# Sums of squares of expert weights moved from ScalarE to GpSimd, and a row of schedule edits, in a one-core attention and PEER kernel

## The chip, the core and the metric

The kernel runs on one core of a Trainium2 chip. TensorE (PE) multiplies matrices into PSUM and takes its stationary operand by a separate weight load (PEld); VectorE (DVE), ScalarE (ACT) and GpSimd (POOL) work element by element on 128 partitions; SyncE (SP) issues most DMAs, and GpSimd issues the indirect ones (gathers). Each engine runs its own instructions in the order in which the program lists them, and semaphores hold an instruction until what it needs is there. The metric is the device time of one execution in microseconds.

## What is computed

```python
def reference(A_x, A_wq, A_wk, A_wv, A_wo, B_x, B_w_q, B_k1, B_k2, B_u, B_v):
    ...                                   # x: 1 x 2048 x 512, 32 heads
    x = A_x
    xn = _layernorm(x, axis=-1)
    return x + _A_ref(xn, A_wq, A_wk, A_wv, A_wo) + _B_ref(xn, B_w_q, B_k1, B_k2, B_u, B_v)

def _A_ref(...):                          # attention, 32 query heads of 16, one key and value head
    scores = jnp.einsum("bhqd,bkd->bhqk", q, k) * (Dh ** -0.5)
    p = _softmax(scores, axis=-1)
    o = jnp.einsum("bhqk,bkd->bhqd", p, v)
    return o ... @ wo

def _B_ref(...):                          # product-key experts, N = 64 * 64 = 4096, D = 512
    q = jnp.einsum("nd,dhc->nhc", xf, w_q)
    s1 = jnp.einsum("nhd,ed->nhe", q1, k1); s2 = jnp.einsum("nhd,ed->nhe", q2, k2)
    i1, i2 = the two best of s1 and of s2; top_e = the two best of their four sums; g = softmax
    act = _gelu(jnp.einsum("nd,nhkd->nhk", xf, u[top_e]))
    out = jnp.einsum("nhk,nhk,nhkd->nd", g, act, v[top_e])
```

## The kernel before

**Two threads on one list.** The program is written out by hand under a manual schedule, so the order of every engine is the order in which the Python code emits. A start of some 115 us normalizes x, makes queries and keys and the first expert weights. Then a main loop of steps `d` emits, in each step, two key blocks of attention (`scores` L448 and its exponential L455, `pv` L465), a function `mid`, and a function `fill` that draws pieces from the generator `score_thread` until a cost budget is used up. Tokens come in four phases of 512.

**Expert scores.** For each of 8 chunks `c` of heads, `wp_make(c)` multiplies raw weights (`wqt`, four tiles `h` of 128 x 1024 f32) with the keys (`pw` L644), transposes them (`pwt` L657) and splits them into a high f16 part `wk[:, 0]` (ACT, L659) and a low one `wk[:, 1]` (DVE, L660). The scale of the split comes from the sum of squares of the chunk's raw weights: `wp_square` (L615) squares one raw tile on ACT and adds it up along the row, `wp_factors` adds four such columns over the partitions with a matmul (L622), reads them on ACT (L624) and makes a power of two on DVE. Chunks 0 and 1 and part of 2 are made in the start, chunks 2 to 7 in the first part of the main loop; from chunk 3 on, the squares are emitted while the chunk before it is split. `item` multiplies a token tile with the chunk (12 matmuls, L699, the terms high-high, high-low, low-high of each of four `k`), and DVE finds the best two (L712, L714). `batch` turns four items into indices on POOL (L758 to L774, or L758 to L806) and gates on DVE.

**Phases 0 and 1: gathers.** 512 "slots" of 128 tokens each fetch one row of u and v per token by an indirect DMA on POOL (L1180, ring `g` of 12 tiles). `dot` (L1192, DVE, both inputs in SBUF) makes the activation, `add` (L1227, DVE, both inputs in SBUF) adds the weighted row. How many slots a step takes is set by a table: `pos` grows by 2.5, 2.3, 1.75, 0.5 and so on, by what the other thread is doing (`dense_on`).

**Phases 2 and 3: dense.** After the last chunk of such a phase, `dense` builds gates with one-hot matrices (`onehot` L973 to L976 on DVE, `pg` L1012 on PE, `dense_on` 2), then runs 32 blocks of experts over all 512 tokens (`pact` L915, `pout` L1058; `dense_on` 3 and 1). `later_split(b)` and `half(b)` split a block's weights (ACT L874, DVE L877); the table `SPLITS` says after which one-hot round. The order of phases is 0, two chunks of 1, 2 with its dense part, the rest of 1, 3 with its dense part.

Of the kernel before, what the change touches and what calls it, by code (L numbers as in the profile page):

```python
# [23 lines left out]
P = 128  # L24
S = 2048
D = 512
# [34 lines left out]
def tile_kernel(ctx, tc, x, wq, wkv, wo, wqT, kT, uv, ub, vb, out):  # L61
# [144 lines left out]
                BULK.append(lambda k=k, xt=xt: nc.sync.dma_start(d_xt[g - 1][k], raw(xt[:])))  # L206

    TERMS = ((0, 0), (0, 1), (1, 0))

    FIRST = ((0, 0), (1, 0), (0, 1))  # L210
    cols = const.tile([P, 40], F32, name="cols")
# [393 lines left out]
        nc.sync.dma_start(w, wqT[4 * c + h].rearrange("(s p) d -> p s d", p=P))  # L605
        WC["raw", c, h] = w

    squares = const.tile([P, 4], F32, name="squares")
    squared, factored = [0], [0]

    def wp_square():
        n = squared[0]
        squared[0] += 1
        junk = big.tile([P, 2, D], BF16, name="junk", tag="wk", bufs=NWK)
        nc.scalar.activation(junk, WC["raw", n // 4, n % 4], AF.Square, accum_out=squares[:, n % 4:n % 4 + 1])  # L615

    def wp_factors():
        c = factored[0]
        factored[0] += 1
        p = xtile("pn")[:, :1]  # L620
        for h in range(4):
            nc.tensor.matmul(p, ones_f, squares[:, h:h + 1], start=h == 0, stop=h == 3)  # L622
        x = small.tile([P, 1], F32, name="xw")
        nc.scalar.activation(x, p, AF.Copy, scale=col(K2))  # L624
        factors(x.bitcast(I32), col(S_W + c), col(I_W + c))
# [4 lines left out]
    def wp_make(c):  # L630

        wt = [big.tile([P, 2, 512], F32, name="wt", tag="da", bufs=2) for _ in range(2)]
        for h in range(4):
            for n in range(4 * c + h + 1, min(4 * c + h + 5, 4 * NC) if late[0] else 4):
                if ("raw", n // 4, n % 4) not in WC:
                    wp_load(n // 4, n % 4)
            if c == 2 and h > 1:
                wp_square()
            if c > 2 and h == 1:
                wp_factors()  # L640
            w = WC.pop(("raw", c, h))
            p = xtile("pw")
            for s in range(2):
                nc.tensor.matmul(p[s * E:(s + 1) * E, :], kTs[:, s, :], w[:, s, :], start=True, stop=True)  # L644
            nc.scalar.copy(wt[h // 2][:, h % 2, :], p)
            yield 0.9
        WC[c] = []
        if c == 2:
            yield 0.05
            wp_factors()  # L650
            yield 0.05
        for k in range(KC):
            for _ in range((0, 2, 1, 1)[k] if 1 < c < NC - 1 else 0):
                wp_square()
            p = xtile("pwt")
            for h in range(4):
                nc.tensor.transpose(p[:, h * P:(h + 1) * P], wt[h // 2][:, h % 2, k * P:(k + 1) * P], ident)  # L657
            wk = wk_tile()
            nc.scalar.activation(wk[:, 0, :], p, AF.Copy, scale=col(S_W + c))  # L659
            low = lambda p=p, wk=wk: nc.vector.scalar_tensor_tensor(wk[:, 1, :], p, col(S_W + c), wk[:, 0, :],  # L660
                                                                    op0=OP.mult, op1=OP.subtract)
            if c == 1 and late[0] is None:
                AFTER.append(low)
            else:
                low()
            WC[c].append(wk)
            (store if c > 1 else BULK.append)(lambda k=k, wk=wk: nc.sync.dma_start(d_w[c][:, k], raw(wk[:])))
            yield 0.45
# [12 lines left out]
    def item(n_, ti, make=()):  # L681
        ph, c = SEQ[n_]
        nph, nc_ = SEQ[n_ + 1] if n_ + 1 < len(SEQ) else (None, None)
        t = TPH * ph + ti
        g, j = divmod(t, GT)
        b, jb = divmod(ti, BT)
        if jb == 0:
            m8 = small.tile([P, BT, 8, 8], F32, name="m8", bufs=1)
            i8 = small.tile([P, BT, 8, 8], U32, name="i8", bufs=1)
            M8[ph, c, b], I8[ph, c, b] = m8, i8  # L690
        m8, i8 = M8[ph, c, b], I8[ph, c, b]
        p = xtile("psc")

        more = nc_ is not None and not (ph >= NSP and c == NC - 1)
        read = more and n_ + 1 >= NC
        n = 0
        for k in range(KC):
            for a, bb in TERMS:
                nc.tensor.matmul(p, XT[k][:, a, j * P:(j + 1) * P], WC[n_][k][:, bb, :],  # L699
                                 start=n == 0, stop=n == 11)  # L700
                n += 1
            if read and ti == 0 and k < 2:
                wp_read(n_ + 1, range(2 * k, 2 * k + 2))
            if k < KC - 1:
                yield 3 * UNIT
            if k == 1 or k == 0 and n_ == 1:

                yield from islice(make, 1)
        if more and nph != ph:
            load_xt(nph, j)  # L710
        for s in range(8):
            nc.vector.max(m8[:, jb, s, :], p[:, s * E:(s + 1) * E])  # L712
        for s in range(8):
            nc.vector.max_index(i8[:, jb, s, :], m8[:, jb, s, :], p[:, s * E:(s + 1) * E])  # L714
        if jb == BT - 1:
            batch(ph, c, b)
        yield 3 * UNIT
# [13 lines left out]
    def batch(ph, c, b):  # L731
# [22 lines left out]
            LATER.append(go)  # L754

        fi = T("fi", F32, [P, BT, 8, 2])
        G_ = nc.gpsimd
        G_.tensor_copy(fi, i8[:, :, :, 0:2])  # L758
        fv = fi.rearrange("p t (h s) k -> p t h s k", s=2)
        i1a, i1b, i2a, i2b = fv[:, :, :, 0, 0], fv[:, :, :, 0, 1], fv[:, :, :, 1, 0], fv[:, :, :, 1, 1]  # L760
# [63 lines left out]
    def dense(DG, after):  # L824
# [144 lines left out]
        def onehot(q):  # L969
            if q < NQ:  # L970
# [6 lines left out]
                OH[q] = oa, ob  # L977

        half = lambda b: on_act(lambda: halves.__setitem__(b, half_split(b, 0)))
        SPLITS = {NQ - 18: lambda: later_split(0), NQ - 15: lambda: later_split(1),  # L980
                  NQ - 12: lambda: half(2), NQ - 10: lambda: later_split(2),
                  NQ - 8: lambda: half(3), NQ - 6: lambda: later_split(3),
                  NQ - 4: lambda: half(4), NQ - 2: lambda: later_split(4)}

        def first_gates():

# [87 lines left out]
        for b in range(NB):  # L1074
            wd = []
            if b > 1:
# [6 lines left out]
                for k in activations(b, splits[b][0], p):  # L1083
                    if k == 0:
                        store(lambda b=b: (fetch_gates(b + 1), fetch_gates(b + 2)))
                        if b % 2 == 0 and b > 2:
                            later_split(b + 2)
                        if b == 2:

                            store(load_totals)  # L1090
# [56 lines left out]
            for _ in range(b - 1 if b in (2, 3) else 0):  # L1147
                if out_ready():
                    block_out()
                    yield 3.6  # L1150
            if b % 2 and b > 1:
                later_split(b + 2)
            if b > 4 and b % 4 == 1 or b == NB - 1:
                n = 4 if b < NB - 1 else 2
# [299 lines left out]
    with tc.manual_schedule(engines=ENGINES):  # L1454
# [34 lines left out]
        def stores(bulk=0):  # L1489
            run(STORES)  # L1490
            for _ in range(min(bulk, len(BULK))):
                BULK.pop(0)()
# [16 lines left out]
        score_steps(4)  # L1509
        norm_stats(2, range(2, GT))  # L1510
        query_squares(0, 3)
        wp_factors()
        zero_m()
        transpose_group(1)
        stores()
        load_group(3)
        score_steps(4)
# [20 lines left out]
        gathers(NGB // 2)  # L1538
        transpose_group(3)
        query_squares(2, 3)  # L1540
        score_steps(2)
        stores(4)
        key_products(3)
# [31 lines left out]
    with tc.manual_schedule(engines=ENGINES):  # L1575
# [6 lines left out]
        for d in range(half + 24):  # L1582
# [2 lines left out]
            if dense_on[0] != 0:  # L1585
                since = d
            if dense_on[0] == 1:
                pos += 2.5 if d < half * 3 // 4 else max(0.0, NSL - pos) / max(half - 3 - d, 1)
            else:
                pos += (2.5 if len(IDX) < NC * TPH else 2.3 if 0 <= d - since < 32 else 1.75, 0, 0.5, 1.5, 0.5)[dense_on[0]]  # L1590

            todo = max(min(int(pos + 0.001), g_next[0]) - d_next[0], 0) if d else 0

# [109 lines left out]
```

## Time and profile before

| what | us |
|---|---|
| three runs | 1809.59, 1815.26, 1810.92 (median 1810.92) |
| the profiled execution | 1814.29, of which the span from first to last instruction is 1812.6 |
| PE busy in the span | 1705.5 |
| DVE busy | 1592.4 |
| ACT busy | 1328.8 |
| POOL busy | 685.1 |

A page of the profile gives each engine's busy time, the chain of work that ended last (followed back from the end, at each step to what released it), and groups of instructions by line: `out<-in` names the tiles, then come count, busy time, mean ns of one and idle time before them. Windows give busy time in a stretch of the span. A line such as L615 is a line of the kernel before. Matmul ends are modelled, so a busy PE isn't a PE at its peak.

### The profile page before, as it was taken

Reading aid. Unit: us, or ns where it says so; the run is one execution under the profiler, and the core shown is the slowest. Engines: PE = TensorE matmul, PEld = TensorE weight load, DVE = VectorE, ACT = ScalarE, POOL = GpSimd, SP = SyncE. Lnnn points to the kernel's source line nnn. Section 1 sums busy time; section 2 is a strip of 40 time slices with the busy share of each in tenths; the row PEclk is TensorE's granted clock in tenths of the full one; section 3 lists DMA queues with packets and bytes.
Section 4 is the critical chain, followed back from the end, with each engine's and each line's share of the span. In section 5 each row is a group of like instructions: output and inputs, shape, how many; then the busy total and the mean of one; then the engine's idle time right before and its main releaser. Section 6 shows DMA issues by size and latency. Waiting matters only on the chain.

```text
span 1812.6 us, 35046 instructions
## 1 busy us (share of the span) xinstructions
PE 1705.5 (94%) x11070; PEld 601.1 (33%) x11070; DVE 1592.4 (88%) x6337; ACT 1328.8 (73%) x1793; POOL 685.1 (38%) x923
## 2 busy tenths in 40 slices
PE   7989998999998889999999999999998899999998
PEld 3433332333333332333333333332333333333332
DVE  7748898999998976899899899999989868989995
ACT  6467787877767886888888666655667877777774
POOL 1034353445543012344344455445541124544440
PEclk9999999999999999999999999999998999999999
DMA  7378788999764567899999976777443789999893
GB/s 260 125 254 308 264 279 282 316 321 324 270 212 139 169 230 260 284 313 341 302 334 345 330 280 237 237 245 245 149 159 131 224 263 293 324 292 332 290 311 114
DMA packets 257273, 470.98 MB, mean 260 GB/s; under 512 B 107316, under 2 KB 118596, under 8 KB 257084
## 3 DMA queue, kind: packets, MB, share of 16 engines
q0 software_dynamic: 73728, 268.47, 43.2%
q1 hardware_dynamic: 182940, 199.59, 34.4%
q8 instruction: 87, 1.43, 0.3%
q14 instruction: 102, 0.84, 0.1%
q10 hardware_dynamic: 416, 0.66, 0.1%
HBM read 407.36 MB, written 56.39 MB: 256 GB/s over the span
## 4 chain that ended last, share of the span: by engine, by line
PE 58%; DVE 20%; ACT 8%; issue 3%; DMA 3%; POOL 1%; SPq 0%; ACTq 0%; DVEq 0%; another core or an unknown queue 0%; POOLq 0%
PE pv L465 17%; PE sc L448 10%; PE psc L699 10%; PE pout L1058 8%; PE pact L915 7%; ACT pt L455 5%; DVE i L714 4%; DVE xa L1227 3%; DVE m L712 3%; DVE g L1192 3%; PE pwo L565 2%; DVE oh L973 2%; PE pw L644 1%; ACT wk L874 1%; DMA rsb<-dinv 1%
## 5 line engine op out<-in xcount | busy, mean ns | idle before, releaser
L455 ACT ACTIVATE pt<-sc 128x1024 f32<-128x1024 f32 x1024 | 990.1, 1026 | 336.6 <-PE sc L448 299.2
L1180 POOL DMA_INDIRECT g<-in_uv_dram,idx x512 | 544.6, 1064 | 896.7 <-DVE xa L1227 367.8
L465 PE MATMUL pv<-pt,vaug 128*32 128x512 f32 x4096 | 503.6, 610 | 0.0
L1227 DVE SCALAR_TENSOR_TENSOR xa<-g,w,xa 128x512 f32<-128x512 f32 x512 | 372.2, 745 | 0.0
L699 PE MATMUL psc<-wk,xt 128*128 128x512 f16 x1536 | 358.4, 381 | 12.5 <-DVE i L714 7.2
L448 PE MATMUL sc<-qa,kaug 64*128 64x512 f16 x2048 | 325.6, 385 | 40.0 <-ACT pt L455 35.3
L1192 DVE CUSTOM_DVE_ANT_0 g<-g,xa 128x512 f32<-128x512 f32 x512 | 334.3, 682 | 2.6 <-DMA g<-in_uv_dram,idx 2.6
L699 PEld LDWEIGHTS <-xt 128*128 128x128 f16 x1536 | 140.9, 98 | 210.9 <-issue 63.0
L448 PEld LDWEIGHTS <-kaug 64*128 64x128 f16 x2048 | 82.0, 94 | 381.7 <-issue 377.9
L714 DVE FIND_INDEX8 i<-m,psc 128x8 uint32<-128x64 f32 x1024 | 206.4, 222 | 0.0
L465 PEld LDWEIGHTS pv<-pt,vaug 128*32 128x32 f32 x4096 | 108.2, 110 | 259.8 <-issue 259.8
L915 PE MATMUL pact<-xt,wk 128*128 128x512 f16 x768 | 184.3, 385 | 4.2 <-DVE wk L877 3.9
L1058 PE MATMUL pout<-wk,wd 128*128 128x512 f16 x768 | 176.5, 380 | 0.0
L712 DVE MAX8 m<-psc 128x8 f32<-128x64 f32 x1024 | 146.1, 214 | 7.9 <-PE psc L699 7.2
L915 PEld LDWEIGHTS <-wk 128*128 128x128 f16 x768 | 69.6, 99 | 105.3 <-issue 29.3
L1058 PEld LDWEIGHTS <-wd 128*128 128x128 f16 x768 | 73.2, 98 | 93.3 <-issue 9.3
L973 DVE TENSOR_TENSOR oh<-io,tr 128x2048 f16<-128x2048 f16 x64 | 77.9, 1218 | 10.0 <-PE pg L1012 4.7
L714 DVE MATCH_VALUE_LOAD i<-m,psc 128x8 f32 x1024 | 72.1, 70 | 0.0
L1131 DVE SCALAR_TENSOR_TENSOR gy<-gy,pact 128x512 f32<-128x512 f32 x60 | 41.0, 683 | 30.2 <-ACT gy L1130 29.0
L1061 DVE SCALAR_TENSOR_TENSOR da<-pout,cols,da 128x512 f32<-128x512 f32 x72 | 53.3, 746 | 15.3 <-PE pout L1058 14.4
L758 POOL CAST fi<-i 128x64 f32<-128x64 uint32 x32 | 8.2, 257 | 141.7 <-DVE i L714 137.9
L1110 DVE SCALAR_TENSOR_TENSOR gy<-gy,gates 128x512 f32<-128x512 f32 x60 | 41.4, 690 | 22.1 <-ACT gy L1132 17.3
(218 smaller groups left out, 1464.6 us busy)
## 6 DMA issues: line engine op xcount, KB each, us to landing
wk<-dw SPq DMA_DIRECT2D x96, 256.0 KB
wqt<-in_wqT_dram SPq DMA_DIRECT2D x32, 512.0 KB
un<-in_uv_dram SPq DMA_DIRECT2D x16, 1024.0 KB
ds<-wk SPq DMA_DIRECT2D x64, 256.0 KB
gates<-dg SPq DMA_DIRECT2D x64, 256.0 KB
wk<-ds SPq DMA_DIRECT2D x64, 256.0 KB
dg<-gst SPq DMA_DIRECT2D x14, 928.0 KB
dw<-wk SPq DMA_DIRECT2D x32, 256.0 KB
```

The source lines that it names most:

```text
L448: nc.tensor.matmul(p[:, b, :], kaug[o:o + 64, kc * P:(kc + 1) * P], QA[u][o:o + 64, i, :], start=True, stop=True)
L455: nc.scalar.activation(PT[u, kc, i], p, AF.Exp, scale=SCALE)
L465: nc.tensor.matmul(PV[u][32 * j:32 * j + 32, :], vaug[:, kc, :], pt[:, b, :], start=kc == 0, stop=kc == 15)
L699: nc.tensor.matmul(p, XT[k][:, a, j * P:(j + 1) * P], WC[n_][k][:, bb, :], start=n == 0, stop=n == 11)
L712: nc.vector.max(m8[:, jb, s, :], p[:, s * E:(s + 1) * E])
L714: nc.vector.max_index(i8[:, jb, s, :], m8[:, jb, s, :], p[:, s * E:(s + 1) * E])
L915: nc.tensor.matmul(p, us[:, a, k * P:(k + 1) * P], XT[k][:, c, :], start=n == 0, stop=n == 11)
L973: nc.vector.tensor_tensor(out=oa, in0=num(P), in1=bc(0, tb, P), op=OP.is_equal)
L1058: nc.tensor.matmul(p, wd[0][:, a, j * P:(j + 1) * P], vs[:, c, :], start=n == 0, stop=n == last)
L1180: nc.gpsimd.indirect_dma_start(out=gt, out_offset=None, in_=uv, in_offset=bass.IndirectOffsetOnAxis(ap=IDX[ph, c, ti][:, s:s + 1], axis=0))
L1192: nc.vector.tensor_tensor_reduce(u, u, XN[TPH * ph + ti], scale=1.0, scalar=0.0, op0=OP.mult, op1=OP.add, accum_out=a[:, i:i + 1])
L1227: nc.vector.scalar_tensor_tensor(acc, v, w[:, i:i + 1], acc, op0=OP.mult, op1=OP.add)
```

## The change

1. `wp_square` runs on GpSimd: one instruction squares a raw tile (f32 in, bf16 out, 128 x 1024), and for the second to fourth tile of a chunk a second one adds the result to the first. A new `wp_sum` on ACT reads the one sum of a chunk along its row (`Copy` with an accumulator); `wp_factors` then has one matmul for each chunk instead of four. That makes 56 GpSimd instructions (32 squares, 24 sums) and 8 ACT instructions in the place of 32 ACT squares. The calls are placed anew: one square for each `k`, `wp_sum` at `h == 1`, `wp_factors` at `h == 3`.
2. In the first item of a chunk (`ti == 0`) the four matmuls that read the low parts of `wk` for `k` 0 to 3 come as late as the table `LOWS_LAST` allows.
3. In phases 2 and 3 the index work of the last chunk (`batch`, 15 instructions) runs on DVE instead of POOL.
4. `SPLITS`: blocks 0 to 3 are split at later one-hot rounds, block 4 no longer there but in block 2's first `k`; block 5 in block 3's first `k` instead of its end.
5. Slots: 2.6 instead of 2.5 for each step in the first dense part, 0.25 instead of 0.5 in the one-hot rounds, 2.3 for 20 steps instead of 32 behind a dense part; what is left goes to the last dense part.

```diff
+    LOWS_LAST = ((0, 0, 0), (0, 1, 0), (1, 0, 0), (1, 1, 0), (2, 0, 0), (2, 1, 0),
+                 (0, 0, 1), (1, 0, 1), (3, 0, 0), (3, 1, 0), (2, 0, 1), (3, 0, 1))
...
-    squares = const.tile([P, 4], F32, name="squares")
-    squared, factored = [0], [0]
+    squares = const.tile([P, 1], F32, name="squares")
+    squared, factored, SUM = [0], [0], [None]
 
     def wp_square():
         n = squared[0]
         squared[0] += 1
-        junk = big.tile([P, 2, D], BF16, name="junk", tag="wk", bufs=NWK)
-        nc.scalar.activation(junk, WC["raw", n // 4, n % 4], AF.Square, accum_out=squares[:, n % 4:n % 4 + 1])
+        w = WC["raw", n // 4, n % 4]
+        sq = big.tile([P, 2, D], BF16, name="sqr", tag="wk", bufs=NWK)
+        nc.gpsimd.tensor_tensor(out=sq, in0=w, in1=w, op=OP.mult)
+        if n % 4:
+            nc.gpsimd.tensor_tensor(out=SUM[0], in0=SUM[0], in1=sq, op=OP.add)
+        else:
+            SUM[0] = sq
+
+    def wp_sum():
+        nc.scalar.activation(SUM[0], SUM[0], AF.Copy, accum_out=squares)
...
-        for h in range(4):
-            nc.tensor.matmul(p, ones_f, squares[:, h:h + 1], start=h == 0, stop=h == 3)
+        nc.tensor.matmul(p, ones_f, squares, start=True, stop=True)
...
-            if c == 2 and h > 1:
+            if c == 2 and 0 < h < 3:
                 wp_square()
             if c > 2 and h == 1:
+                wp_sum()
+            if c > 2 and h == 3:
                 wp_factors()
...
         if c == 2:
+            wp_sum()
             yield 0.05
             wp_factors()
             yield 0.05
         for k in range(KC):
-            for _ in range((0, 2, 1, 1)[k] if 1 < c < NC - 1 else 0):
+            if 1 < c < NC - 1:
                 wp_square()
...
-            for a, bb in TERMS:
-                nc.tensor.matmul(p, XT[k][:, a, j * P:(j + 1) * P], WC[n_][k][:, bb, :],
+            for kk, a, bb in LOWS_LAST[n:n + 3] if ti == 0 else [(k, *ab) for ab in TERMS]:
+                nc.tensor.matmul(p, XT[kk][:, a, j * P:(j + 1) * P], WC[n_][kk][:, bb, :],
...
-        G_ = nc.gpsimd
+        G_ = V if ph >= NSP and c == NC - 1 else nc.gpsimd
...
-        SPLITS = {NQ - 18: lambda: later_split(0), NQ - 15: lambda: later_split(1),
-                  NQ - 12: lambda: half(2), NQ - 10: lambda: later_split(2),
-                  NQ - 8: lambda: half(3), NQ - 6: lambda: later_split(3),
-                  NQ - 4: lambda: half(4), NQ - 2: lambda: later_split(4)}
+        SPLITS = {NQ - 16: lambda: later_split(0), NQ - 12: lambda: later_split(1),
+                  NQ - 9: lambda: half(2), NQ - 8: lambda: later_split(2),
+                  NQ - 6: lambda: half(3), NQ - 5: lambda: later_split(3)}
...
-                        if b % 2 == 0 and b > 2:
+                        if b % 2 == 0 or b == 3:
                             later_split(b + 2)
...
-            if b % 2 and b > 1:
+            if b % 2 and b > 3:
                 later_split(b + 2)
...
-                pos += 2.5 if d < half * 3 // 4 else max(0.0, NSL - pos) / max(half - 3 - d, 1)
+                pos += 2.6 if d < half * 3 // 4 else max(0.0, NSL - pos) / max(half - 3 - d, 1)
             else:
-                pos += (2.5 if len(IDX) < NC * TPH else 2.3 if 0 <= d - since < 32 else 1.75, 0, 0.5, 1.5, 0.5)[dense_on[0]]
+                pos += (2.5 if len(IDX) < NC * TPH else 2.3 if 0 <= d - since < 20 else 1.75, 0, 0.25, 1.5, 0.5)[dense_on[0]]
```

In the start, the calls of `wp_square` stay where they were; a `wp_sum` is put in front of `zero_m()` and in front of the `score_steps(2)` behind `query_squares(2, 3)`, and the first `wp_factors` comes behind `transpose_group(1)` instead of in front of `zero_m()`.

Where instructions move is seen from the order of each engine. GpSimd in the main loop, at the index work behind the third chunk's items (`fi`, `e_`, `idx` are its tiles, `i_` the indices that DVE found, `g` the gathers); before, the index work is followed by nine gathers, and thirteen gathers stand in front of it:

```order
L758 CAST fi<-i_2202 128x64
L767 TENSOR_SCALAR fi<-fi 128x16x2
L768 TENSOR_TENSOR e_2603<-fi 128x16
L769 TENSOR_TENSOR e_2604<-fi 128x16
L770 TENSOR_TENSOR fi<-fi 128x16
L771 TENSOR_TENSOR e_2603<-e_2603,e_2604 128x16
L772 TENSOR_TENSOR e_2603<-e_2603,cond 128x16
L773 TENSOR_TENSOR fi<-e_2603,e_2604 128x16
L774 CAST idx<-fi 128x32
L1180 DMA g<-in_uv_dram,idx 128x1024 x9
```

The same place in the change (its line numbers are some 12 higher; `sqr` are the squares, `wqt` the raw weights):

```order
L770 CAST fi<-i_2208 128x64
L779 TENSOR_SCALAR fi<-fi 128x16x2
L780 TENSOR_TENSOR e_2609<-fi 128x16
L781 TENSOR_TENSOR e_2610<-fi 128x16
L782 TENSOR_TENSOR fi<-fi 128x16
L783 TENSOR_TENSOR e_2609<-e_2609,e_2610 128x16
L784 TENSOR_TENSOR e_2609<-e_2609,cond 128x16
L785 TENSOR_TENSOR fi<-e_2609,e_2610 128x16
L786 CAST idx<-fi 128x32
L618 TENSOR_TENSOR sqr<-wqt 128x1024
L620 TENSOR_TENSOR sqr<-sqr 128x1024
L1191 DMA g<-in_uv_dram,idx 128x1024 x7
```

In front of it there now stand ten gathers, two squares and a sum, three gathers, and a square and a sum; the chunk's fourth square and its sum stand behind the index work and in front of the next seven gathers.

ScalarE at the same place, from the exponentials (`pt`) behind that chunk's split (`wk`) on; `wt` are copies of the next chunk's products, `xw` is the factor's read, `ex` and `gth` belong to gates and gathered slots. Before:

```order
L455 ACTIVATE pt<-sc 128x1024 x4
L645 COPY wt<-pw 128x512
L624 ACTIVATE xw<-pn,cols 128x1
L645 COPY wt<-pw 128x512
L455 ACTIVATE pt<-sc 128x1024 x2
L1208 ACTIVATE gth<-gy 128x4
L751 ACTIVATE ex<-mx,cols 128x16
L455 ACTIVATE pt<-sc 128x1024 x2
L645 COPY wt<-pw 128x512 x2
```

and in the change:

```order
L457 ACTIVATE pt<-sc 128x1024 x4
L656 COPY wt<-pw 128x512
L625 ACTIVATE sqr,squares<-sqr 128x1024
L656 COPY wt<-pw 128x512
L457 ACTIVATE pt<-sc 128x1024 x2
L1219 ACTIVATE gth<-gy 128x4
L763 ACTIVATE ex<-mx,cols 128x16
L457 ACTIVATE pt<-sc 128x1024 x2
L656 COPY wt<-pw 128x512
L633 ACTIVATE xw<-pn,cols 128x1
```

The read of the sum (`sqr,squares<-sqr`) stands where the factor's read `xw` stood, in front of the next exponentials, and `xw` two copies later.

On VectorE the number of dots (L1192) between landmarks shows the slots: up to the first one-hot matrix 134 before and in the change; in the first one-hot rounds 8, now 4; from the first item batch behind the first dense part to the second one-hot matrix 93, now 85; in the second one-hot rounds 8, now 4; from the first block sum of the last dense part to the end 125, now 135. Of the block splits (L877) eight halves stood between the first one-hot matrices, now six.

More of the change, by code (lines that the diff above doesn't have):

```diff
@@ L1511, in tile_kernel @@
         query_squares(0, 3)
-        wp_factors()
+        wp_sum()
         zero_m()
         transpose_group(1)
+        wp_factors()
         stores()
@@ L1540, in tile_kernel @@
         query_squares(2, 3)
+        wp_sum()
         score_steps(2)
```

## The prediction

> **What bounds the kernel now.** I read the page's busy times first, then windows by stage, then the chain of waits and the waits of PE in the stages that the change touches.
>
> ```profile
> PE 1705.5 (94%) x11070; PEld 601.1 (33%) x11070; DVE 1592.4 (88%) x6337; ACT 1328.8 (73%) x1793; POOL 685.1 (38%) x923
> ```
>
> On average PE leads and POOL is idle for 62%. The windows (columns: length, busy of PE, PEld, DVE, ACT, POOL, clock, DMA share, GB/s) show different limits:
>
> ```profile
> 120.00:320.00 200.00, 185.90 (x1149) 64.09 (x1150) 173.72 (x881) 157.09 (x230) 89.43 (x114) 0.98 0.83 283
> ...
> 540.00:660.00 120.00, 100.35 (x1048) 40.07 (x1048) 111.72 (x301) 96.06 (x122) 25.46 (x42) 0.94 0.49 162
> 660.00:1030.00 370.00, 351.16 (x2114) 117.46 (x2110) 316.07 (x737) 296.84 (x404) 134.76 (x125) 0.98 0.93 308
> ...
> 1155.00:1345.00 190.00, 183.64 (x1118) 61.42 (x1118) 186.95 (x1194) 114.81 (x141) 97.31 (x181) 0.99 0.66 215
> 1345.00:1450.00 105.00, 88.33 (x1003) 36.01 (x1003) 90.50 (x170) 86.36 (x106) 18.07 (x24) 0.93 0.51 163
> 1450.00:1812.00 362.00, 354.70 (x2107) 118.88 (x2099) 301.01 (x729) 265.08 (x350) 137.49 (x128) 1.00 0.85 278
> ```
>
> DVE is full in 1155:1345 (186.95 of 190) and nearly so in the first one-hot stage (540:660); the two dense stages run at PE's pace; 120:320, where chunks 2 to 7 are made, has PE at 93% and DVE at 87%. The chain in 120:320 says what ACT's squares cost there:
>
> ```profile
> by line: PE psc L699 23.3%; PE pv L465 18.3%; PE sc L448 11.9%; PE pw L644 9.6%; ACT pt L455 8.3%; DMA rsb<-dinv 6.8%; issue 4.8%; ACT junk L615 3.7%; PE pwt L657 2.9%; PE pn L622 2.6%; DVE wk L660 1.5%; ACT wk L659 1.5%; DVE xa L1227 1.0%;
> ```
>
> L615 has 3.7% of 200, or 7.4 us: that is the most that taking squares off ACT can bring in this stage.
>
> **What a GpSimd square costs.** No row has this instruction. The nearest:
>
> ```profile
> L354 POOL MEMSET g<- 128x1024 f16 x1 | 1.0, 951 | 0.0
> ...
> L797 POOL TENSOR_TENSOR e<-fi x32: 208/216/725, 419.1 to 1346.8; 128x16 f32<-128x16 f32 x32
> ...
> L798 POOL TENSOR_TENSOR e<-e,cond x32: 220/588/787, 419.4 to 1347.1; 128x16 f32<-128x16 f32 x32
> ...
> L803 POOL TENSOR_TENSOR da<-hi,ii x32: 246/250/493, 423.6 to 1349.2; 128x32 f32<-128x32 f32 x32
> ```
>
> A write of 1024 elements takes 0.95 us: the lower end. The shortest two-input instructions take 208 or 220 ns for 16 elements and 246 for 32, so 1.6 to 2.4 ns for each element, and 246 + 992 of them make 1.9 to 2.6 us. I take 2.2 us, since these rows are the same operation; the 56 instructions are then 123 us. The Trainium skill, GPSIMD Engine Reference, section 3.1, states 4497 ns for 2048 f32 elements of `tensor_tensor`, which makes 2.25 us an estimate for 1024; the sum below would be the same by it.
>
> **What it does to DVE.** The same rows span 220 to 787 ns for one shape, so something holds them. The timeline shows what, in both directions (start, duration):
>
> ```profile
> 478.31 0.24 POOL L758 CAST fi<-i 128x64 f32<-128x64 uint32 x1 [6.83 <-DVE i L714]
> 478.34 0.26 DVE L741 TENSOR_TENSOR c<-m 128x16 f32<-128x16 f32 x1
> ...
> 563.67 0.79 POOL L798 TENSOR_TENSOR e<-e,cond 128x16 f32<-128x16 f32 x1
> ...
> 563.69 0.69 DVE L1192 CUSTOM_DVE_ANT_0 g<-g,xa 128x512 f32<-128x512 f32 x1
> ...
> L741 DVE TENSOR_TENSOR c<-m x32: 170/181/263, 85.9 to 1344.5; 128x16 f32<-128x16 f32 x32
> ```
>
> POOL's L798 ends at 564.46, just behind the DVE dot that ended at 564.38. And DVE's L741, which takes 181 ns at the median, takes 260 when POOL's cast began 0.03 us ahead of it, and ends 0.05 us after it. So a GpSimd instruction that reads SBUF and a DVE instruction with two SBUF inputs don't run side by side: the second waits for the first. With 16 or 64 elements on POOL's side that costs DVE under 0.1 us; with 2.2 us it costs up to 2.2. Dots and adds are such instructions:
>
> ```profile
> L1227 DVE SCALAR_TENSOR_TENSOR xa<-g,w,xa 128x512 f32<-128x512 f32 x512 | 372.2, 745 | 0.0
> ...
> L1192 DVE CUSTOM_DVE_ANT_0 g<-g,xa 128x512 f32<-128x512 f32 x512 | 334.3, 682 | 2.6 <-DMA g<-in_uv_dram,idx 2.6
> ```
>
> The Trainium skill, SBUF — State Buffer, "Who interferes with whom", says that the one issued second "fully blocks", and that DVE's `tensor_scalar` in a 2-port mode does so too, which no row here shows; by that the four normalizations of the start (L184) would wait as well and the start below would be some 3 us worse, an estimate.
>
> **Sum, 120:320.** Of the 56 instructions 39 fall here (4 for chunk 2, then 5 chunks of 7). POOL issues gathers right behind DVE's adds, and the squares behind the gathers, so they meet DVE's next dots. A stall lasts from nothing (DVE in best-two searches) to 2.2 us; I take half: 39 x 1.1 = 43 us. DVE then needs 173.7 + 43 = 217 us; at the 98.4% to which 1155:1345 fills it that is 220, so **+20**. Second, ACT's read of the sum waits for POOL in front of exponentials:
>
> ```profile
> 199.40 0.54 POOL L774 CAST idx<-fi 128x32 int32<-128x32 f32 x1
> ...
> 203.03 0.26 ACT L624 ACTIVATE xw<-pn,cols 128x1 f32<-128x1 f32 x1 [0.93 <-PE pn L622]
> ```
>
> The fourth square and its sum start behind that cast, at 199.9, and end at 204.4 or, held by DVE, 205; ACT would read at about 202. Behind it two exponentials and PE's `pv` queue. Five times 2 to 3 us are 12, of which DVE's delay covers half: **+6**. Gathers come later by up to 9 us, with POOL at 89 + 86 of 200; they are twelve tiles ahead, which I take as cover; without it the first dots of a chunk would wait some 2 us each. ACT's 7.4 us and part 2 of the change (PE's waits for a low part, below) are gains on a path that no longer ends last: 0. Ends: 0 (0.95 us each, 18 us of stalls in DVE's 26 idle ones) and +45 (every stall whole, partly absorbed).
>
> ```profile
> PE psc L699 <- DVE wk L660: 3.9, 3, 2.0
> ```
>
> **Sum, start.** Chunk 0's seven instructions need only the loads:
>
> ```profile
> 10.72 1.92 SPq L605 DMA_DIRECT2D wqt<-in_wqT_dram  x4
> ...
> 16.86 2.74 DVE L1486 SCALAR_TENSOR_TENSOR wqs<-g,cols,wqs 128x512 f16<-128x512 f32 x4
> ...
> 19.86 5.34 PE L274 MATMUL pq<-xt,wqs 128*128 128x512 f16 x24
> ```
>
> Loads issued at 10.7 land some 4 us later, so POOL works from 15 to past 30 us, across DVE's four two-input splits of `wqs`, which PE's query products need at 20.7 (the fifth matmul, 5.34/24 = 0.22 us each). Each may wait up to 2.2 us: 8.8; they have 1.1 us to spare. I take **+7** (0 to 12) with chunk 1 and the three instructions ahead of the branch. ACT loses 8 squares there: **-2** (PE is seldom waiting for ACT; -4 to 0).
>
> **Sum, the other edits.** One-hot rounds: each stage loses four dots and about as many adds, 4 x (682 + 745) ns = 5.7 us, the first also two half splits. DVE is the limit for most of them: **-10** for both (-13 to -4). Between the dense part and the second one-hot stage eight dots and about six adds go, 8 x 0.68 + 6 x 0.745 and small ones = 11 us, most of them in 1155:1345; DVE is full there but PE has only 6 us idle: **-7** (-11 to -3). The ten dots appear in the last dense stage, +14 us for DVE at 301 of 362, beside PE; four in the first: **+4** (0 to 14).
>
> ```profile
> PE ptd L940 <- POOL da L806: 6.0, 2, 3.4
> ...
> PE pact L915 <- DVE wk L877: 3.9, 1, 3.9
> ```
>
> The index work on DVE ends PE's 6.0 us of waiting for POOL, but puts 2 x 15 instructions of some 0.18 us (L741's median), 5.4 us, on DVE: **-1** (-4 to +3). Block 5's split comes most of a block sooner: **-3** of 3.9 (-4 to 0).
>
> Sum: 20 + 6 + 7 - 2 - 10 - 7 + 4 - 1 - 3 = **+14 us**. The profiled execution took 1814.3 (span 1812.6), 3.4 above the median 1810.9; applied to the median, the forecast is **1825 us**.
>
> **Rivals.** *Faster: the stalls vanish in slack.* If a GpSimd instruction holds the reading side for only about 1 us, or falls mostly beside DVE's searches, DVE's 26 idle us in 120:320 take all of it, and the read on ACT hardly waits. Then 120:320 costs 0 and gets back about 4 of the 7.4 and 3.9 us above; with the start at +7 and the other edits at -2 - 10 - 7 + 4 - 1 - 3 = -19 the sum is -16: 1795. For it: POOL's short instructions hardly slow DVE. Against: L741 waits until POOL's whole instruction is over.
> *About equal.* If stalls cost 12 instead of 26, or gains come out as reckoned but the start loses nothing, all lies within 5 us of 1811.
> *Slower still: POOL becomes the limit.* 89 busy + 86 + waits for half a dot, 39 x 0.35, are 189 of 200 even without pauses between gathers; if the gathers' lead is used up, dots wait for DMAs and 120:320 grows by some 45 us: 1845. It decides from about 2.5 us for each instruction.
> *The slots don't do what they say:* the ten dots moved to the last dense stage cost there what they saved (+14 instead of +4): 1835.
>
> **Numbers.** Forecast with its neighbours above (slower) 0.63: the forecast itself 0.46 (own range 1817 to 1838), POOL as the limit 0.09, slots 0.08. Equal 0.15. Faster 0.22. A change of 0.3%, 5.4 us, is what a measurement can tell: below 1805.5 is faster, above 1816.4 slower. The range 1795 to 1848 leaves out about 0.1 at each end.
>
> **What would show it.** Right: groups for `sqr` at about 2.2 us and longer; dots and adds (L1192, L1227 before) with means above 682 and 745 in 120:320 alone; that stretch 20 us or more longer with DVE near 98%; ACT waiting for POOL at the sums; `wqs` splits spread over 8 us in the start; one-hot stages 5 us shorter each. Wrong: dots at their old means under squares, or squares near 1 us; then 1795 to 1800. If the one-hot stages keep their length, the gains fail and the time goes above 1835.

## The result and the profile after

The changed kernel takes 1843.99 us (median of four runs, 1841.53 to 1846.87); the kernel before, beside it, 1812.19 (1809.59 to 1815.26). The ratio is 1.0174, with a 95% interval of 1.0153 to 1.0194: **slower by 32 us** (28 to 35), where the forecast was 14.

The page of the changed kernel, busy time of each engine:

```profile
PE 1711.3 (93%) x11022; PEld 598.5 (32%) x11022; DVE 1653.5 (90%) x6367; ACT 1305.8 (71%) x1745; POOL 796.1 (43%) x949
```

DVE is busy 61 us longer with almost the same instructions (6337 before), and PE 6 us longer with 48 fewer. Where that happened is seen from windows cut at the same events in both kernels: the last query product (the end of the start), the first index work behind chunk 2 to 7 (the seventh batch), and the first and last one-hot round. First the kernel before (start, chunk stage, gathers, first one-hot stage), then the changed kernel (columns as in the prediction: length; PE, PEld, DVE, ACT, POOL; granted clock, DMA share, GB/s):

```profile
0.00:115.40 115.40, 97.78 (x466) 45.90 (x466) 74.13 (x254) 62.28 (x113) 14.28 (x41) 0.99 0.61 208
115.40:334.30 218.90, 203.03 (x1254) 70.71 (x1253) 189.06 (x958) 173.64 (x255) 94.77 (x119) 0.98 0.82 279
334.30:568.50 234.20, 226.60 (x1395) 77.67 (x1393) 227.75 (x1455) 173.40 (x237) 115.88 (x221) 1.00 0.82 277
568.50:666.30 97.80, 80.55 (x955) 32.98 (x955) 91.31 (x164) 82.85 (x104) 8.27 (x7) 0.94 0.53 179
```

```profile
0.00:125.00 125.00, 101.23 (x454) 46.92 (x454) 86.08 (x254) 54.83 (x98) 45.04 (x56) 0.95 0.56 191
125.00:391.30 266.30, 216.53 (x1218) 69.81 (x1217) 238.24 (x958) 157.61 (x221) 181.07 (x161) 0.88 0.68 229
391.30:625.70 234.40, 227.22 (x1395) 77.00 (x1393) 229.56 (x1471) 173.90 (x238) 110.83 (x204) 0.99 0.82 276
625.70:719.30 93.60, 80.39 (x953) 33.13 (x954) 84.57 (x147) 81.41 (x100) 4.52 (x4) 0.95 0.46 156
```

The start is 9.6 us longer, **the chunk stage 47.4**, the gathers after it 0.2; from there on the changed kernel gains 26 back. In the chunk stage DVE has 49 us more for the same 958 instructions, PE 13.5 us more for 36 fewer, and neither is full (238.2 and 216.5 of 266.3). The granted clock is 0.88, where it was 0.98.

GpSimd's new instructions, and DVE's dots (L1203) and adds (L1238):

```profile
L618 POOL TENSOR_TENSOR sqr<-wqt 128x1024 bf16<-128x1024 f32 x32 | 63.2, 1984 | 19.8 <-DMA wqt<-in_wqT_dram 9.3 <-ACT pt L457 8.6 <-issue 1.6
L620 POOL TENSOR_TENSOR sqr<-sqr 128x1024 bf16<-128x1024 bf16 x24 | 55.1, 2294 | 1.9
...
L1203 DVE CUSTOM_DVE_ANT_0 g<-g,xa 128x512 f32<-128x512 f32 x72 | 68.5, 987 | 0.0
L1238 DVE SCALAR_TENSOR_TENSOR xa<-g,w,xa 128x512 f32<-128x512 f32 x67 | 52.2, 800 | 0.0
```

The first two rows are of the whole span, the last two of the chunk stage alone: there a dot (L1203) takes 987 ns at the mean, where the page of before had 682. What PE and ACT wait for in the stage (waits: total, times, longest):

```profile
PE psc L711 <- DVE wk L672: 16.7, 7, 5.8
PE sc L450 <- ACT pt L457: 11.0, 6, 4.2
...
ACT pt L457 <- PE sc L450: 38.1, 33, 5.8
ACT sqr L625 <- POOL sqr L620: 22.2, 4, 7.3
ACT wt L656 <- PE pw L655: 17.2, 12, 5.8
```

The timeline shows how one such wait comes about:

```profile
296.93 3.75 POOL L618 TENSOR_TENSOR sqr<-wqt 128x1024 bf16<-128x1024 f32 x2
...
298.34 2.89 DVE L1203 CUSTOM_DVE_ANT_0 g<-g,xa 128x512 f32<-128x512 f32 x1
...
299.95 1.46 PE L711 MATMUL psc<-wk,xt 128*128 128x512 f16 x6
...
300.75 2.46 POOL L620 TENSOR_TENSOR sqr<-sqr 128x1024 bf16<-128x1024 bf16 x1
...
301.16 2.60 DVE L1203 CUSTOM_DVE_ANT_0 g<-g,xa 128x512 f32<-128x512 f32 x1
...
305.30 0.75 DVE L672 SCALAR_TENSOR_TENSOR wk<-pwt,cols,wk 128x512 f16<-128x512 f32 x1
...
306.10 1.44 PE L711 MATMUL psc<-wk,xt 128*128 128x512 f16 x3 [4.25 <-DVE wk L672]
...
308.18 1.94 ACT L457 ACTIVATE pt<-sc 128x1024 f32<-128x1024 f32 x2 [5.61 <-PE sc L450]
```

Two dots in a row are held until GpSimd is through. The low split (L672) queued behind them comes 4 us late, PE waits 4.25 for it, and the exponentials 5.61 for PE. Then PE's three matmuls take 0.48 us each, where six a little earlier took 0.24 (299.95, 1.46 us): the clock has dropped (its records show half clock from 304.17 to 311.00). A hold on DVE is thus handed on from engine to engine; that is the reading that the runs had to test.

### The profile page after: what moved, and what is told of

It is laid out like the page before. It is cut to its first block, busy times and chain, and to the rows that moved or that the text cites. A ratio compares the mean times of both kernels' runs of the same rounds, so it can differ in the third digit from the quotient of the medians.

```text
span 1843.3 us, 34966 instructions
## 1 busy us (share of the span) xinstructions
PE 1711.3 (93%) x11022; PEld 598.5 (32%) x11022; DVE 1653.5 (90%) x6367; ACT 1305.8 (71%) x1745; POOL 796.1 (43%) x949
## 4 chain that ended last, share of the span: by engine, by line
PE 46%; DVE 32%; ACT 6%; issue 4%; POOL 2%; DMA 2%; SPq 0%; another core or an unknown queue 0%; ACTq 0%; DVEq 0%; POOLq 0%
PE pv L467 14%; PE sc L450 8%; PE pout L1069 7%; DVE i L726 7%; PE pact L927 7%; PE psc L711 6%; DVE xa L1238 5%; DVE g L1203 5%; DVE m L724 5%; ACT pt L457 4%; DVE oh L985 2%; PE pwo L567 2%; DMA gates<-dg 1%; POOL sqr L620 1%; DVE obs L988 1%
## 5 line engine op out<-in xcount | busy, mean ns | idle before, releaser
L711 PE MATMUL psc<-wk,xt 128*128 128x512 f16 x1536 | 361.4, 384 | 18.0 <-DVE wk L672 16.7
L1238 DVE SCALAR_TENSOR_TENSOR xa<-g,w,xa 128x512 f32<-128x512 f32 x512 | 377.7, 754 | 0.1
L1203 DVE CUSTOM_DVE_ANT_0 g<-g,xa 128x512 f32<-128x512 f32 x512 | 356.4, 726 | 14.2 <-DMA g<-in_uv_dram,idx 14.1
L726 DVE MATCH_VALUE_LOAD i<-m,psc 128x8 f32 x1024 | 76.6, 75 | 0.5 <-DVE i L726 0.5
L618 POOL TENSOR_TENSOR sqr<-wqt 128x1024 bf16<-128x1024 f32 x32 | 63.2, 1984 | 19.8 <-DMA wqt<-in_wqT_dram 9.3
L1142 DVE SCALAR_TENSOR_TENSOR gy<-gy,pact 128x512 f32<-128x512 f32 x60 | 40.8, 680 | 17.6 <-ACT gy L1141 17.1
```

Of the source, the lines that this page charges most:

```text
L711: nc.tensor.matmul(p, XT[kk][:, a, j * P:(j + 1) * P], WC[n_][kk][:, bb, :], start=n == 0, stop=n == 11)
L1203: nc.vector.tensor_tensor_reduce(u, u, XN[TPH * ph + ti], scale=1.0, scalar=0.0, op0=OP.mult, op1=OP.add, accum_out=a[:, i:i + 1])
L1238: nc.vector.scalar_tensor_tensor(acc, v, w[:, i:i + 1], acc, op0=OP.mult, op1=OP.add)
```

## The experiments

Ratios are against the kernel before, run beside each kernel; "us" is (ratio - 1) x 1811. The intervals are some 0.002 (4 us) to either side.

| kernel | median us | ratio (95%) | us |
|---|---|---|---|
| changed | 1843.99 | 1.0174 (1.0153–1.0194) | +32 |
| e1: squares back on ACT, other edits kept | 1787.83 | 0.9852 (0.9832–0.9871) | -27 |
| e2: squares on GpSimd, other edits undone | 1871.30 | 1.0306 (1.0284–1.0327) | +55 |
| e3: changed, memsets for squares and sums | 1822.84 | 1.0039 (1.0017–1.006) | +7 |
| e4: changed, sum read later | 1842.69 | 1.016 (1.0135–1.0185) | +29 |
| e5: as e4, pieces unshifted | 1827.47 | 1.0102 (1.0085–1.0119) | +18 |
| e6: e3 and e5 together | 1791.38 | 0.9912 (0.9894–0.993) | -16 |
| e7: changed, half the width | 1797.86 | 0.9942 (0.9925–0.9958) | -11 |
| e12: e5, each instruction as two halves | 1837.06 | 1.0164 (1.0147–1.0181) | +30 |
| e8: e1, slots undone | 1802.48 | 0.9966 (0.9949–0.9982) | -6 |
| e9: e1, splits undone | 1789.60 | 0.9908 (0.9892–0.9925) | -17 |
| e10: e1, low parts undone | 1781.82 | 0.9857 (0.984–0.9873) | -26 |
| e11: e1, index work undone | 1780.52 | 0.9846 (0.9819–0.9873) | -28 |

### Which part loses: e1, e2

e1 takes part 1 of the change back (`wp_square`, `wp_factors` and their places as before); e2 puts part 1 alone into the kernel before.

> The changed kernel with the squares taken back to ScalarE (four columns, four matmuls, the old places); all other edits stay. Theory A (all of the loss comes with the GpSimd squares): from the marks of the two traces, 9.6 us in the start and 47.4 between the last query product and the seventh batch, so 1844 - 57 = 1787, and at most 1793. Rival (the low parts put last, or another edit, cost part of the 47 in the stage where chunks are made): 1800 or more, with that stage still over 10 us longer than before.

> The kernel before with the GpSimd squares alone. Theory A: 1812 + 57 = 1869, with the marks of start and chunk stage as in the changed kernel (+9.6 and +47). Rival (other edits share in the loss): below 1855.

Measured: 1787.8 and 1871.3. By the ratios the squares cost 58 us on top of the other edits and 55 without them, and the other edits bring 27: they simply add up, and **e1 beats both kernels**. The chunk stage of e1 (windows):

```profile
115.00:331.40 216.40, 199.87 (x1254) 70.64 (x1253) 188.90 (x958) 173.54 (x255) 95.59 (x119) 1.00 0.82 282
```

It is 2.5 us shorter than before, so no other edit shares in the 47 us. That this trace never loses clock there is a matter of one execution: in e8, e9 and e11 below, which have the same chunk stage, it is 217 to 218 us, with 7 to 10 of them at half clock (7 before).

### How the squares lose: e3 to e6

Two suspects: the hold on DVE, and ACT's wait for GpSimd's sum in front of exponentials. e3 takes away the hold (memsets read nothing), e4 the wait.

```diff
-        nc.gpsimd.tensor_tensor(out=sq, in0=w, in1=w, op=OP.mult)
+        nc.gpsimd.memset(sq, 0.01)
+        nc.gpsimd.memset(sq, 0.01)
...
-            nc.gpsimd.tensor_tensor(out=SUM[0], in0=SUM[0], in1=sq, op=OP.add)
+            nc.gpsimd.memset(SUM[0], 0.01)
+            nc.gpsimd.memset(SUM[0], 0.01)
```

```diff
-            if c > 2 and h == 1:
-                wp_sum()
             if c > 2 and h == 3:
-                wp_factors()
+                wp_sum()
...
             yield 0.05
+        if c > 1:
             wp_factors()
             yield 0.05
```

> The changed kernel with each GpSimd square and each GpSimd sum replaced by two memsets of the same tile (to 0.01, whose sum over a row is near the real one); the squares themselves are left out. GpSimd is busy about as long (2 x 0.95 for 1.9 to 2.3 us) and ScalarE still waits for it, but GpSimd reads nothing. Theory H (GpSimd's reading holds VectorE): dots fall back from 0.726 to about 0.68 us, and the time to 1790 to 1805. Rival Q (GpSimd's time itself, gathers behind it and ScalarE's waits for it): the time stays above 1830.

> The changed kernel with the sum read at h == 3 instead of h == 1 from chunk 3 on, and the factors behind the fourth tile; everything is computed. ScalarE's waits for GpSimd's sums (25.9 us in 5) should fall below 6. Theory H: the dots stay at 0.726 us, and the time falls by 5 to 15, to 1829 to 1839. Rival S (ScalarE's wait in front of exponentials is the main loss): it falls by 20 or more, below 1824. If it doesn't fall at all, that wait was covered.

Neither theory of e3 came out: 1822.8 lies between. The dots were back at 0.69 us, so GpSimd's reading is the hold (the memsets don't wait for the raw weights either; the stage times below contain that difference); but ACT now waited 28.5 us for the sums, and the stage was still 248.2. e4 took ACT's waits in the stage down to 4.6 us and shortened it to 256.2, but the kernel ended where the changed one did. e4 has one more `yield` for each chunk, so the pieces of `wp_make` fall between other items; e5 does the same without it (its diff against the changed kernel follows), and e6 is e5 with the memsets of e3, so that both suspects are gone:

```diff
-            if c > 2 and h == 1:
-                wp_sum()
             if c > 2 and h == 3:
-                wp_factors()
+                wp_sum()
...
+        elif c > 2:
+            wp_factors()
         for k in range(KC):
```

> The changed kernel with the sum read at h == 3 from chunk 3 on, as in the last of the runs before, but the factors without a piece of their own, so that the pieces fall where they did; everything is computed. In that run the chunk stage (last query product to seventh batch) took 256.2 instead of 266.4 us, and the gain was gone by the one-hot rounds. If the shifted pieces gave it back there: the stage at about 256 and the end at 1831 to 1836. Rival (what is gained here is lost behind whatever the order): 1840 to 1844.

> The late sum as above, and each GpSimd square or sum as two memsets (to 0.01; the squares are left out), so that GpSimd reads nothing and ScalarE does not wait for it, with GpSimd as busy as before. If the hold on VectorE and ScalarE's wait are all of the loss: a chunk stage of 216 to 224 us (216.4 with the squares on ScalarE), the half clock there below 10 us of time (34 with the memsets alone, 61 in the changed kernel), and 1794 to 1802 in all, with the start some 6 late. Rival (GpSimd's time itself, by gathers that come later, or the ring of tiles that the sums hold): the stage above 235 and the end above 1810.

e5 kept its gain: 1827.5, a little better than expected. e6 came to 1791.4, below its range, with GpSimd nearly as busy as in the changed kernel (ACT still waited 7.7 us for two sums). So GpSimd's own time, later gathers and the ring of tiles cost 1 to 4 us (219.9 for 216 to 219 with the squares on ACT); the half clock was 13.7 us there, not below 10. The chunk stages of e3, e5 and e6, in this order (windows):

```profile
122.00:370.20 248.20, 208.12 (x1218) 68.25 (x1217) 189.18 (x958) 157.51 (x221) 165.61 (x197) 0.93 0.73 246
```

```profile
124.80:377.10 252.30, 211.03 (x1218) 69.21 (x1217) 236.47 (x958) 157.63 (x221) 180.98 (x161) 0.93 0.72 242
```

```profile
119.70:339.60 219.90, 201.85 (x1219) 68.15 (x1218) 189.73 (x959) 157.61 (x221) 165.92 (x197) 0.97 0.81 278
```

| chunk stage, us | early read of the sum | late read |
|---|---|---|
| GpSimd reads (hold) | 266.3 (changed) | 252.3 (e5) |
| GpSimd only writes | 248.2 (e3) | 219.9 (e6) |

The hold alone costs 32.4 (252.3 - 219.9), the wait alone 28.3, both 46.4. Behind the hold the wait still costs 14.0. And PE's busy time falls with the clock's loss: 216.5, 211.0, 208.1 and 201.9 us for the same work (changed, e5, e3, e6) at 0.88, 0.93, 0.93 and 0.97. The clock's records put the time at half clock in the stage at 61, 38, 34 and 14 us.

### How the hold depends on the size of an instruction: e7, e12

e7 against the changed kernel, then e12 against e5; the sums likewise, and in e7 also ACT's read:

```diff
-        nc.gpsimd.tensor_tensor(out=sq, in0=w, in1=w, op=OP.mult)
+        nc.gpsimd.tensor_tensor(out=sq[:, 0], in0=w[:, 0], in1=w[:, 0], op=OP.mult)
```

```diff
-        nc.gpsimd.tensor_tensor(out=sq, in0=w, in1=w, op=OP.mult)
+        for i in range(2):
+            nc.gpsimd.tensor_tensor(out=sq[:, i], in0=w[:, i], in1=w[:, i], op=OP.mult)
```

> The changed kernel with squares and sums over the first half of each raw tile (128 x 512); the other half of the sum of squares is left out. Each GpSimd instruction then takes about 1.0 to 1.2 us. If the loss goes with how long each instruction holds VectorE: the dots' surplus falls to half or less (0.70 us mean at most), VectorE's busy time in the chunk stage from 238 to about 212 us (189 without squares on GpSimd), the stage to about 235, and the end to 1808 to 1818. Rival (the loss goes with the number of instructions or with the place of ScalarE's read): above 1830.

> The kernel with the late sum in unshifted pieces (1827.5), with each GpSimd square and sum as two instructions of half the width; everything is computed. The held time in all is the same or a little more (two times 1.09 for 1.98 us, two times 1.31 for 2.35), and VectorE can go between the halves. If the loss goes with the held time in all: 1822 to 1835. Rival (it goes with the length of a single hold, since half the width over half the tile cost only 10 us against the kernel without GpSimd squares): 1812 or less, with a chunk stage below 238 us (252.3 with whole instructions).

e7 came to 1797.9, better than expected. DVE's busy time in the stage rose by 17.6 us against e1 (206.5 for 188.9; 212 was expected), the dots' surplus fell to less than half (8.9 for 21.7 us), and the stage grew by only 11.3, to 227.7, though ACT still waited 14.9 us for the sums. So half the width costs about a quarter of what the whole does: the loss grew faster than the instruction. The hold and ACT's wait both fell here, so that this isn't the hold alone.

That made shorter instructions look like the cure. e12 came to 1837.1, slower than e5 with whole instructions and 2 us above the range of the first theory, with a stage of 262.1 us for 252.3. The halves are no cure; but what failed is the premise of both theories, that DVE goes between them. The timeline of e12 shows it, GpSimd's rows first:

```profile
337.89 2.04 POOL L619 TENSOR_TENSOR sqr<-wqt 128x512 bf16<-128x512 f32 x2
339.89 2.26 POOL L622 TENSOR_TENSOR sqr<-sqr 128x512 bf16<-128x512 bf16 x2
342.11 2.02 POOL L619 TENSOR_TENSOR sqr<-wqt 128x512 bf16<-128x512 f32 x2
344.11 2.26 POOL L622 TENSOR_TENSOR sqr<-sqr 128x512 bf16<-128x512 bf16 x2
```

```profile
340.19 6.73 DVE L1205 CUSTOM_DVE_ANT_0 g<-g,xa 128x512 f32<-128x512 f32 x1
```

One dot takes 6.73 us: it is issued in the middle of a run of eight halves that follow each other without a gap, and ends 0.55 us behind the last. DVE didn't get in between these halves. It isn't always so: from 147.31 on, in the same trace, DVE and GpSimd take turns half by half, and three dots in a row take 1.47 to 1.63 us. But in the chunk stage of e12 ten DVE instructions waited beyond the half that they met, and these make 40 of the 54 us that held instructions there took longer; in e5 none did, in the changed kernel one (the dot at 298.34, through two squares; it came in ahead of the sum at 300.75). So e12 made the holds longer, not shorter, and says nothing against the length of a hold as the cause. What decides whether DVE gets in wasn't tried.

### The other edits one at a time: e8 to e11

Each undoes one of them in e1: the numbers of the slots; `SPLITS` and block 5's place; `LOWS_LAST`; the engine of the last chunk's index work.

> The kernel with the squares on ScalarE and all other edits (1787.8), with the slots put back to 2.5, 0.5 and 32 steps. By the prediction's sum the slots bring 5 in each one-hot stage and 7 in the stretch behind the first dense part, and cost 4 in the dense ones: 1787.8 + 13 = 1801, at least 1796. Rival (the moved dots and adds cost where they land what they saved): 1785 to 1791.

> The kernel with the squares on ScalarE and all other edits (1787.8), with SPLITS and block 5's split put back. By the prediction block 5's split is worth 3, and the two half splits that leave the first one-hot stage up to 4: 1791 to 1795. Rival (worth nothing, the slots did it all): 1787 to 1789.

> The kernel with the squares on ScalarE and all other edits (1787.8), with the four low parts of a chunk's first item back in their order. The prediction counted them at nothing: 1786 to 1790. Rival (PE's waits for a low part, 3.9 us in the kernel before, come back as time, and with them half clock, of which the kernel with the edit has none in the chunk stage and the kernel before 6.8 us): 1791 to 1795.

> The kernel with the squares on ScalarE and all other edits (1787.8), with the index work of the last chunk of phases 2 and 3 back on GpSimd. The prediction has it at 1 us: 1787 to 1790. Rival (the 6.0 us in which PE waited for GpSimd's index work in the kernel before were time, with half clock behind them): 1793 to 1798.

The medians of the kernel before were 1814.06 beside e1, 1810.23 beside e8 and 1807.80 beside e9 to e11, so that ratios are compared, not times. Against e1's ratio, undoing the slots costs 21 us and the splits 10 (each some 5 to either side; the profiled spans give 17 and 8); the low parts and the index work come out at 1 and -1. The slots are worth what was expected or more. The splits come out above either theory, though with their 5 to either side they touch the first one's 3 to 7; the bare time of e9 lies within 1 us of the rival's range. Most of their gain isn't in the one-hot rounds: between the first `pact` matmuls behind the first rounds and the first `pout` e9 takes 52.3 us, where e1, e10, e11 and the changed kernel all take 46.7 or 46.8, and it takes 2 more in the blocks right behind. The index work saves nothing; by the traces PE only changes whom it waits for: 6.0 us for POOL in the kernel before, and in the changed one for DVE:

```profile
PE ptd L952 <- DVE da L829: 3.3, 2, 2.1
...
PE ptd L952 <- DVE da L818: 1.2, 1, 1.2
PE ptd L952 <- DVE gy L940: 1.2, 1, 1.2
```

The stretch between the first dense part and the second one-hot stage, and that one-hot stage, before and in e1:

```profile
1049.60:1344.30 294.70, 288.34 (x1734) 96.59 (x1727) 287.17 (x1764) 181.35 (x222) 152.34 (x251) 0.99 0.68 226
1351.70:1447.00 95.30, 81.36 (x954) 33.48 (x954) 86.06 (x156) 79.37 (x99) 12.30 (x9) 0.93 0.56 177
```

```profile
1032.80:1317.30 284.50, 284.07 (x1723) 96.04 (x1722) 277.59 (x1734) 179.76 (x217) 146.68 (x245) 1.00 0.67 224
1325.70:1414.40 88.70, 75.35 (x953) 31.85 (x951) 83.24 (x147) 78.79 (x96) 10.71 (x7) 1.00 0.53 174
```

In the first, 9.6 us less of DVE made 10.2 us, and PE is full now. In the second, 2.8 us less of DVE made 6.6, with the clock back from 0.93 to 1.00 and PE's busy time down by 6 for the same matmuls.

## Why the prediction was right and wrong

The direction, the place and the mechanism were right, the size was not: +14 was forecast, +32 measured. By the terms below the squares were forecast at +31 (20 + 6 + 5) and cost 55 to 58 (e2, e1); the other edits, which brought 9 more than forecast, hid a part of that.

| term | forecast | measured |
|---|---|---|
| a GpSimd instruction | 2.2 us | 1.98 and 2.29 |
| added to DVE in the chunk stage | 43 | 47 (e5 236.5, e6 189.7) |
| that, on the path | +20 | **+32** (e5 against e6) |
| ACT's read of the sum | +6 | **+14** (changed against e5) |
| ACT's 7.4 us and low parts | 0 | +1 (e6 against before) |
| start | +5 | **+9.6** |
| other edits behind the chunk stage | -17 | **-26** (marks of the changed kernel) |

**The chunk stage is the step that failed.** "DVE then needs 173.7 + 43 = 217 us; at the 98.4% to which 1155:1345 fills it that is 220": the 43 was right (41 instructions, not 39, held DVE for 1.14 us each at the mean in e5, where 1.1 was taken), the 98.4% didn't hold here. With the surplus measured, 236.5/0.984 is 240; e5 took 252.3, a fill of 93.7%, and the changed kernel 266.3, a fill of 89%. In 1030:1350 of the kernel before, around the stretch from which the fill was taken, PE waited 5.3 us for DVE, and DVE 3 for ACT. In e5's chunk stage PE waited 27 us for DVE (16.0 of them for low splits), and DVE 7 for ACT's high parts and 5 for PE. The fill of the one didn't carry over to the other. "Five times 2 to 3 us are 12, of which DVE's delay covers half": the waits were 22.2 us in four, up to 7.3, and little covered them: e5 took 16.7 us of them away and the stage lost 14.0, and from e3 to e6 20.8 less of waits made 28.3. The cover had been assumed, not read from a row. What neither term had is the clock: the changed kernel's stage is 48 to 50 us longer than that of e1, e8, e9 and e11, and 13 to 17 of these are PE's busy time, which went up with the half clock; the rest are pauses. No run took the clock away by itself. The Trainium skill, TensorE: Matmul & The Clock Gate, Part 1 (The HAM clock gate), has the array at half rate behind an idle window of some 3.4 us; here shorter pauses sufficed (last point of the last section).

The rival "POOL becomes the limit" gave 1845, nearly the time that came, by a mechanism that wasn't there: POOL is at 181 of 266, and e6, with POOL at 166 of 220, loses next to nothing. "The stalls vanish in slack" is refuted by e5 against e6 (32.4 us for the hold). "The slots don't do what they say" is refuted by e8.

**The start.** The four splits of `wqs` went from 2.74 to 8.34 us, as the prediction said they could:

```profile
16.85 8.34 DVE L1497 SCALAR_TENSOR_TENSOR wqs<-g,cols,wqs 128x512 f16<-128x512 f32 x4
```

```profile
20.18 1.46 PE L276 MATMUL pq<-xt,wqs 128*128 128x512 f16 x6
22.95 0.39 PE L276 MATMUL pq<-xt,wqs 128*128 128x512 f16 x1 [1.32 <-DVE wqs L1497]
25.25 6.72 PE L276 MATMUL pq<-xt,wqs 128*128 128x512 f16 x17 [1.91 <-DVE wqs L1497]
```

PE's query products (second fence) lose 3.2 us of pauses, and then 17 matmuls at 0.40 us instead of 0.22, 3 us more. Where the other 3 of the 9.6 us come from wasn't followed, nor was the gain of 2 for ACT's squares seen by itself. **The other edits** had the right signs, and the slots and splits the right places; their surplus of 9 us came in the stretch behind the first dense part (10 us for 8) and in the first dense part, which became 8 us shorter where 3 were counted; 4.6 of the 8 are PE's busy time, with the clock back from 0.98 to 1.00. The last dense part didn't lose what was counted there: it is as long as before (364.5 us for 365.0) with the ten moved slots in it.

## What to carry to other kernels

Work moved to an idle engine isn't free where its instructions hold those of the bound engine, as GpSimd's two-input ones did here with DVE's: multiply their count by the hold, and then ask who waits for the instruction queued behind the held one. In a stage where engines hand work to each other, don't divide the busy time by the best fill seen elsewhere; take each wait at its price unless a row shows the cover, and count what PE's pauses cost in clock. Two waits in the same stage are best priced by taking away each and both.

## What the runs showed of the hardware

- **A run of GpSimd instructions can hold DVE to its end.** In a run of eight half-width instructions back to back a dot took 6.73 us, and a sixteen-element instruction 7.32 (e12, 180.21); in others DVE came in behind one half (147.31, 1.47 us). The Trainium skill, SBUF — State Buffer, "SBUF: two separate sides", gives the shared pair to whichever starts first "for the whole instruction"; that agrees with the whole-width dots of 2.6 us, and the 6.73 goes further than the page.
- **Some one-input DVE instructions are held too.** The prediction had no row for it. In the start of the changed kernel a `TENSOR_SCALAR` of two elements took 1.09 us, beside GpSimd's sum, and ended with it; in e1 (second fence) it takes 0.17. One of a single element, issued right ahead of it beside the same sum, wasn't held (0.14 us), and in the whole trace 57 index searches that began inside a square or a sum weren't either:

```profile
24.72 2.44 POOL L620 TENSOR_TENSOR sqr<-sqr 128x1024 bf16<-128x1024 bf16 x1
...
25.99 0.14 DVE L342 TENSOR_SCALAR cols<-cols 128x1 f32<-128x1 f32 x1
26.11 1.09 DVE L344 TENSOR_SCALAR most<-most 128x2 int32<-128x2 int32 x1
```

```profile
20.75 0.17 DVE L344 TENSOR_SCALAR most<-most 128x2 int32<-128x2 int32 x1
```

- **GpSimd's memsets don't hold dots**: in e3 and e6 the dots that began beside a memset of 0.95 us took 0.70 us at most.
- **The clock goes by how busy PE was, in steps of 3.41 us; short pauses add up.** Two pauses of 1.32 and 1.91 us in the start of the changed kernel went with 6.83 us at half clock, from 24.28 on. The Trainium skill, TensorE: Matmul & The Clock Gate, Part 1, speaks of an idle window of 3.4 us; here PE was busy for 34% of the 3.41 us ahead of the drop. The clock's records last 3.41 us or a multiple of it. Cut along these steps, the fourteen traces (from 20 us on) hold 159 drops to half clock: PE had been busy for at most 57% of the step ahead of each, and no step below 44% kept the full clock. Ahead of all 159 returns PE had been busy for at least 82% of the step. (The ends of matmuls are modelled, so these shares are rough.)
